# Linear attention and expert layer on one core: key features as the stationary side, z from a column of ones, logits from transposes, key subtractions on GpSimd

## The chip, the core and the metric

The kernel runs on one core of a Trainium2 chip. A core has a matrix engine (TensorE, PE; its weight loads are shown apart as PEld), a vector engine (VectorE, DVE), an engine for activations (ScalarE, ACT), a general one (GpSimd, POOL), and a queue engine (SyncE, SP) that issues most of the transfers between the device memory and the on-chip memory. Matrix products land in PSUM, eight banks of 128 x 512 f32. The engines run their own instructions in order and wait for each other by semaphores. The metric is the device time of one execution in microseconds.

## The reference

```python
def phi(x):
    proj = np.einsum('bhsd,df->bhsf', x, w_phi)
    proj = proj - np.max(np.abs(proj), axis=-1, keepdims=True)
    return np.concatenate([np.exp(proj), np.exp(-proj)], axis=-1)
q_p, k_p = (phi(q), phi(k))
kv = np.einsum('bhsf,bhsd->bhfd', k_p, v)
z = np.sum(k_p, axis=2)
num = np.einsum('bhsf,bhfd->bhsd', q_p, kv)
den = np.einsum('bhsf,bhf->bhs', q_p, z)[..., None] + 1e-06
attn = num / den                      # 8 batches, 8 heads, 576 tokens, 64 wide
x = attn.transpose(0, 2, 1, 3).reshape(4608, 512)
logits = x @ w_gate                   # 8 experts
...
out[mask] = np.maximum(x[mask] @ w1[e], 0.0) @ w2[e]
```

Projections have 128 features, so a head's feature vector has 256. The tokens are given to the experts in order of all logits, each expert taking at most 576; the left-out lines do that.

## The kernel before

The attention comes first, then the expert part (`moe`), whose instructions the change leaves alone. The attention has 16 units; a unit is two heads (a) of two batches (i). Its steps, with the names that the profile shows:

- SP loads keys and queries in pieces (ki, qi; eight transfers each) and values (vi; two transfers, one for each batch, with a row of 9 x 64 values in one piece). DVE transposes the 32 x 32 blocks (kT, qT, L158).
- Projection (L169): three groups of three token columns for keys and three for queries, each in a pair of PSUM banks. For each, DVE takes the maximum of the absolute values (kgm, qgm, L173) and subtracts it (kgt, qgt, L176), which frees the banks.
- Keys: ACT makes both exponentials (kP, L188). GpSimd adds kP up over the nine token columns (ks, L194 and L195), for z. PE multiplies (L204): the values are the stationary side, 64 x 64, and 256 features move past it. ACT copies the product (kvT, L208); PE multiplies it by a block that holds a unit matrix and the gate's weights (bd, L220), which turns it round and makes eight logit columns; ACT copies that into kz (L223). PE sums ks over the partitions (L235), and DVE copies the result into the 73rd column of kz (L237).
- Queries: PE transposes the features (L248), ACT makes the exponentials (qP, L252).
- Numerator (L265), in two halves g of five and four token columns: 73 columns, that is 64 values, 8 logits and the denominator. DVE divides (rd, xp, L269 to L280), SP stores xp into xs (L284), and GpSimd adds the logit columns into L (L290, L292); the last unit's are added by DVE.

Between them DVE makes constants (L353 to L414, of patterns that GpSimd makes) and, once a pair of batches is done, some steps of the routing (L424 to L478), with a count on PE (L474).

The order of all these steps is settled when the program is built: the class `Plan` is a list scheduler that knows for each step its engine, an estimated duration, the steps it needs, the buffers it takes and frees, and a due time. It takes the step with the earliest start on its engine and, among those ready, the one with the earliest due time, with an extra cost where PE would change its tile shape (mode). The due times are the unit's number times TI plus a constant for each kind of step, from the table ATT in the last lines. The step functions are then called in that order, so each engine's instructions stand in the planned order. PSUM is dealt out in four pairs of banks (kind 'g').

Of the kernel before, what the change touches and what calls it, by code (L numbers as in the profile page):

```python
# [89 lines left out]
def attention(ctx, tc, nc, q, k, v, w_phi, w_gate, xs, L, C, xp, cfg={}, after=None, later=None, count=None, init=iter(())):  # L90
# [24 lines left out]
    def loadv(u):  # L115
        bp,hp=divmod(u,NP)
        t=T['v',u]=sb.tile([128,2,9,D],F32,name='vi',bufs=2)
        for i in range(2):
            o=bass.AP(tensor=v.tensor,offset=v.offset+((2*bp+i)*H+2*hp)*HS,ap=[[9*D,64],[HS,2],[1,9*D]])
            nc.sync.dma_start(t[64*i:64*i+64].rearrange('p h s d -> p h (s d)'),o)  # L120
# [17 lines left out]
    def unit(u):  # L138
        bp,hp=divmod(u,NP)
        t0=u*d['TI']  # L140
        def add(name,eng,dur,due,fn,deps=(),mode=None,slot=(),frees=(),lat=None,after=0.):
            P.add((name,u),eng,dur,t0+due,fn,[(x,u) for x in deps],
                  lat={'PE':170.,'DVE':95.,'ACT':100.,'POOL':30.,'SP':0.}[eng] if lat is None else lat,mode=mode,slot=slot,frees=frees,after=after)
        def slots(*l): return tuple((kd,n,(kd,u) if len(z)==0 else (kd,u)+tuple(z)) for kd,n,*z in l)
        first=u==0
# [7 lines left out]
        def blocks(nm,aft):  # L153

            for bi in range(2):
# [3 lines left out]
                add((nm+'t',bi),'DVE',640.,d[nm+'t']+.7*bi,f,['ld'+nm],slot=slots((nm+'T',2)) if bi==0 else (),frees=((nm+'i',u),),after=aft[bi] if first else 0.)  # L159
        def project(nm,g,s0,s1,due,src):  # L160
# [13 lines left out]
            def sub(x):  # L174
                t=T[nm+'t',u,g]=sb.tile([128,2,n,128],F32,name=nm+'t',bufs=3)
                V.tensor_sub(t,vw(),T[nm+'m',u,g].to_broadcast([128,2,n,128]))  # L176
# [4 lines left out]
        blocks('k',(7500.,8500.))
        for g,(s0,s1) in enumerate(SG):
# [7 lines left out]
            def ad(x,s0=s0,s1=s1,g=g):  # L190
                if g==0: T['ks',u]=sb.tile([128,2,256],F32,name='ks',bufs=2)
                ks=T['ks',u]; kP=T['kP',u]
                for s in range(s0,s1):
                    if s==1: G.tensor_add(ks,kP[:,0],kP[:,1])  # L194
                    elif s>1: G.tensor_add(ks,ks,kP[:,s])  # L195
            add(('ad',g),'POOL',1300.*(n-(g==0)),due+4.,ad,[('ke',g)]+([('ad',g-1)] if g else []),frees=(('kP',u),),slot=slots(('ks',2)) if g==0 else ())
            def kv(x,s0=s0,s1=s1,g=g):
                if g==0: T['kvp',u]=pair(('g',u,'kv'))(x)
                p=T['kvp',u]; kP=T['kP',u]; v_=T['v',u]
                for s in range(s0,s1):  # L200
                    for i in range(2):
                        r=slice(64*i,64*i+64)
                        for a in range(2):
                            PE.matmul(p[64*a:64*a+64,i,0:256],v_[r,a,s,:],kP[r,s,a,:],start=s==0,stop=s==8,skip_group_check=True)  # L204
            add(('kv',g),'PE',n*430.+40.,d['kv']+d['kvs']*g,kv,[('ke',g)]+([('kv',g-1)] if g else ['ldv']),'Q',slots(('g',NG,'kv')) if g==0 else (),(('kP',u),('vi',u)))
        def kvt(x):
            t=T['kvT',u]=sb.tile([128,2,256],F32,name='kvT',bufs=2)
            A.copy(t,T['kvp',u][:,:,0:256])  # L208
        kend=d['kv']+2*d['kvs']+1.5
        add('kvt','ACT',ac(512),kend,kvt,[('kv',2)],frees=(('g',u,'kv'),))  # L210
        def bd(x):
            p=T['bdp',u]=pair(('g',u,'bd'))(x)
            t=T['kvT',u]
            for i in range(2):
                for fh in range(2):
                    for a in range(2):
                        r=slice(64*a,64*a+64)
                        for c in range(2):
                            o=128*fh+64*c
                            PE.matmul(p[64*c:64*c+64,a,72*(2*i+fh):72*(2*i+fh)+72],t[r,i,o:o+64],C['bd'][r,hp,:],start=True,stop=True)  # L220
        def kz(x):
            t=T['kz',u]=sb.tile([128,2,2,2,73],F32,name='kz',bufs=2)
            A.copy(t.rearrange('p i h a e -> p a (i h) e')[:,:,:,0:72],T['bdp',u][:,:,0:288].rearrange('p a (g e) -> p a g e',e=72))  # L223
        add('bd','PE',520.,kend+d['bd'],bd,['kvt'],'Q',slots(('g',NG,'bd')))
        add('kz','ACT',ac(576),kend+d['bd']+.6,kz,['bd'],slot=slots(('kz',2)),frees=(('g',u,'bd'),))
        def z(x):
            p=T['zp',u]=pair(('g',u,'z'))(x)
            ks=T['ks',u]
            for a in range(2):
# [26 lines left out]
        for g,(j0,j1) in enumerate(JG):  # L256
# [9 lines left out]
            def dve(x,g=g,j0=j0,j1=j1,n=n):  # L266
# [7 lines left out]
                if lastu:  # L274
                    V.tensor_mul(x_[:,:,j0:j1,64:72],p[:,:,:,64:72],rd.to_broadcast([128,2,n,8]))
# [637 lines left out]
```

## Time and profile before

| | |
|---|---|
| median of 3 runs | 811.54 us (810.16 to 812.07) |
| the profiled execution | 809.45 us, its span 807.7 us |
| PE busy | 756.6 us (94% of the span) |
| DVE busy | 573.1 us (71%) |
| ACT busy | 327.3 us (41%) |
| POOL busy | 263.8 us (33%) |
| mean granted clock of PE | 0.975 |

Busy times are counted over the whole span, in which the attention takes a good third; a share of the whole says little about one of the two parts. In the rows of the timeline and of the groups, L and a number is a line of the kernel, the names behind the operation are the tile written and those read, and x and a number is the count of instructions. A matrix product in f32 shows two records for each call in the code, so a group of 12 calls is shown as x24; the transposes show one. [...]

### The profile page before, as it was taken

What the parts mean: (1) busy time and instruction counts of PE and PEld (TensorE: products, weight loads), DVE (VectorE), ACT (ScalarE), POOL (GpSimd) and SP (SyncE); (2) the same over time, 40 slices, a digit from 0 to 9 for tenths busy, and PEclk for the clock granted to TensorE, in tenths of its full rate; (3) what the DMA queues carried; (4) which work ended last, traced back from release to release, by engine and by line L of the source; (5) the groups of instructions that cost most, each with busy time, mean ns of one, the idle gap of its engine ahead of it and who ended that gap; (6) DMA issues with size and microseconds to landing.
All of it is one profiled execution on the core that took longest, in us unless ns stands there. A gap on an engine that the chain in (4) does not pass through costs nothing.

```text
span 807.7 us, 25190 instructions
## 1 busy us (share of the span) xinstructions
PE 756.6 (94%) x10718; PEld 653.4 (81%) x10718; DVE 573.1 (71%) x1407; ACT 327.3 (41%) x579; POOL 263.8 (33%) x295
## 2 busy tenths in 40 slices
PE   5888999999999996799999999999999999999995
PEld 3777887888888785488798798798898898897983
DVE  5798899999999885787686686586586685550400
ACT  2544555665554463143343243234334333441410
POOL 2664676655666560200401302203103104302011
PEclk9999999999999997699999999999999999999998
DMA  8868668668777311433424314405314424701300
GB/s 130 146 119 161 119 121 155 128 118 165 126 152 143 77 33 32 134 135 116 128 83 144 127 58 161 161 16 180 138 54 137 138 89 131 271 1 45 119 27 32
DMA packets 225344, 91.89 MB, mean 114 GB/s; under 512 B 191905, under 2 KB 208321, under 8 KB 225233
## 3 DMA queue, kind: packets, MB, share of 16 engines
q1 hardware_dynamic: 214400, 70.74, 37.5%
q0 software_dynamic: 6096, 18.97, 7.0%
q8 instruction: 84, 1.38, 0.7%
q10 hardware_dynamic: 4736, 0.59, 0.5%
q14 instruction: 28, 0.22, 0.1%
HBM read 71.39 MB, written 18.87 MB: 112 GB/s over the span
## 4 chain that ended last, share of the span: by engine, by line
PE 58%; issue 14%; DVE 10%; POOL 5%; SPq 5%; DMA 4%; ACT 3%; POOLq 0%; DVEq 0%; ACTq 0%
PE h L788 19%; PE y L817 17%; PE g L265 5%; SPq L114 4%; PE g L204 3%; PE g L169 3%; POOL ks L195 3%; PE y L832 2%; PE g L248 2%; ACT qP L252 2%; DMA qi<-in_q_dram 2%; PE h L763 2%; POOL out_dram L846 1%; PE rps L541 1%; DMA ki<-in_k_dram 1%
## 5 line engine op out<-in xcount | busy, mean ns | idle before, releaser
L195 POOL TENSOR_TENSOR ks<-ks,kP 128x512 f32<-128x512 f32 x112 | 142.8, 1275 | 9.9 <-ACT kP L188 1.3
L788 PE MATMUL h<-xh,w1h 128*128 128x272 f32 (+3 forms) x512 | 144.5, 303 | 0.2 <-DVE xl L766 0.2
L788 PE MATMUL h<-xh,w1l 128*128 128x272 f32 (+3 forms) x512 | 143.0, 299 | 0.0
L846 POOL DMA_INDIRECT out_dram<-ysb,idx x40 | 40.4, 1010 | 206.2 <-ACT ysb L840 166.7
L799 ACT ACTIVATE fh<-h 128x272 fp32r<-128x272 f32 (+2 forms) x128 | 49.2, 384 | 134.8 <-PE h L788 123.6
L817 PE MATMUL y<-w2h,fl 128*128 128x512 f32 x256 | 102.2, 399 | 0.0
L817 PE MATMUL y<-w2l,fh 128*128 128x512 f32 x256 | 101.9, 398 | 0.0
L817 PE MATMUL y<-w2h,fh 128*128 128x512 f32 x256 | 101.5, 397 | 0.0
L788 PEld LDWEIGHTS h<-xh,w1h 128*128 128x128 f32 x512 | 96.5, 189 | 2.1 <-issue 1.2
L758 POOL DMA_INDIRECT xg<-xs,idx x40 | 39.5, 987 | 177.2 <-issue 141.3
L788 PEld LDWEIGHTS h<-xh,w1l 128*128 128x128 f32 x512 | 96.7, 189 | 0.0
L803 DVE SCALAR_TENSOR_TENSOR fl<-h,fh 128x272 fp32r<-128x272 f32 (+2 forms) x128 | 52.8, 420 | 55.8 <-ACT fh L799 42.4
L788 PE MATMUL h<-xl,w1h 128*128 128x272 f32 (+3 forms) x512 | 91.8, 298 | 0.0
L188 ACT ACTIVATE kP<-kgt 128x768 f32<-128x768 f32 x96 | 74.5, 835 | 32.9 <-DVE kgt L176 32.5
L265 PE MATMUL g<-kz,qP 128*64 128x73 f32 x2304 | 77.6, 227 | 3.9 <-issue 2.1
L265 PEld LDWEIGHTS g<-kz,qP 128*64 128x64 f32 x2304 | 74.9, 136 | 7.6 <-issue 4.2
L252 ACT ACTIVATE qP<-g 128x768 f32<-128x768 f32 x96 | 71.9, 820 | 11.2 <-PE g L248 11.1
L788 PEld LDWEIGHTS h<-xl,w1h 128*128 128x128 f32 x512 | 75.6, 189 | 0.0
L204 PE MATMUL g<-kP,vi 64*64 64x256 f32 x1152 | 69.7, 382 | 2.4 <-DVE xp L280 1.3
L840 ACT COPY ysb<-y 128x512 f32<-128x512 f32 (+1 forms) x40 | 21.8, 544 | 101.1 <-PE y L817 70.9
L204 PEld LDWEIGHTS g<-kP,vi 64*64 64x64 f32 x1152 | 48.1, 135 | 13.8 <-issue 2.1
L194 POOL TENSOR_TENSOR ks<-kP 128x512 f32<-128x512 f32 x16 | 20.5, 1280 | 109.2 <-ACT kP L188 109.2
(179 smaller groups left out, 1329.2 us busy)
## 6 DMA issues: line engine op xcount, KB each, us to landing
raww<-in_moe_w_dram SPq DMA_DIRECT2D x64, 512.0 KB, 6.2
vi<-in_v_dram SPq DMA_DIRECT2D x32, 288.0 KB, 4.6
xs<-xp SPq DMA_DIRECT2D x32, 288.0 KB, 3.8
ki<-in_k_dram SPq DMA_DIRECT2D x124, 72.0 KB, 3.2
qi<-in_q_dram SPq DMA_DIRECT2D x124, 72.0 KB, 3.3
xg<-xs,idx POOLq DMA_INDIRECT x40, 3.6
out_dram<-ysb,idx POOLq DMA_INDIRECT x40, 3.5
ki<-in_k_dram ACTq DMA_DIRECT2D x4, 72.0 KB, 5.3
```

Source lines behind the costliest of these rows:

```text
L114: eng.dma_start(t[64*a+32*db:64*a+32*db+32,bi],o)
L188: for i in range(2): A.activation(o[:,:,:,128*i:128*i+128],t,AF.Exp,scale=1.0-2*i)
L195: elif s>1: G.tensor_add(ks,ks,kP[:,s])
L204: PE.matmul(p[64*a:64*a+64,i,0:256],v_[r,a,s,:],kP[r,s,a,:],start=s==0,stop=s==8,skip_group_check=True)
L252: for fh in range(2): A.activation(t[:,fh].rearrange('p a s t -> p a (s t)'),p,AF.Exp,scale=1.0-2*fh)
L265: PE.matmul(p[64*ab:64*ab+64,a,73*(j-j0):73*(j-j0)+73],T['qP',u,j//3][:,fh,a,j%3,64*ab:64*ab+64],T['kz',u][:,ab,fh,a,:],start=fh==0,stop=f ...
L758: G.indirect_dma_start(out=T['xg',r][0:n,bb,:],out_offset=None,in_=xs,in_offset=bass.IndirectOffsetOnAxis(ap=T['idx',r][0:n,bb,:],axis=0))
L788: PE.matmul(p,ws[:,k,o:o+128],xx[:,k,o1:o2],start=n==0,stop=n==11)
L799: A.activation(hh[:,f,o1:o1+m1],p[:,0:m1],AF.Relu)
L803: V.scalar_tensor_tensor(hl[:,f,o1:o1+m1],p[:,0:m1],0.0,hh[:,f,o1:o1+m1],op0=OP.max,op1=OP.subtract)
L817: PE.matmul(p,hx[:,f,o:o+128],ws[:,f%2,:],start=n==0,stop=n==23)
L846: st=G.indirect_dma_start(out=ov,out_offset=bass.IndirectOffsetOnAxis(ap=iv,axis=0),in_=yv,in_offset=None)
```

## The change

The key-value product has its sides exchanged: the features kP are stationary, in 64 x 64 pieces, and the values move, 64 columns and a 65th of ones, so that z comes out with the product. It is made of four steps of 9 token columns (one for each half of the features and head), and the first now needs all three groups of kP. GpSimd's sums, the product with bd, the product for z and DVE's copy fall away. The ones stand in two fixed value tiles; the values are loaded in four transfers a unit, each with rows of 64 values in a piece.

The logit columns are made from the product in kz: PE transposes its four blocks (tv), ACT copies them (tc), PE multiplies them by the gate's weights (gl, 16 columns), and ACT copies the eight columns that belong to each head beside its values (gc). In kz the two heads of a block now share their neighbourhood of columns: logits, ones and values of the one (columns 0 to 72), values, ones and logits of the other (73 to 145), and the code behind it takes the denominator, values and logits from other columns.

The keys' subtraction of all three groups goes from DVE to GpSimd: ACT copies the projection from PSUM into kgt, DVE still takes the maximum from PSUM, and GpSimd subtracts in place.

```diff
-    def loadv(u):
+    def loadv(u,b):
         bp,hp=divmod(u,NP)
-        t=T['v',u]=sb.tile([128,2,9,D],F32,name='vi',bufs=2)
+        t=T['v',u]=VI[b]
         for i in range(2):
-            o=bass.AP(tensor=v.tensor,offset=v.offset+((2*bp+i)*H+2*hp)*HS,ap=[[9*D,64],[HS,2],[1,9*D]])
-            nc.sync.dma_start(t[64*i:64*i+64].rearrange('p h s d -> p h (s d)'),o)
+            for a in range(2):
+                o=bass.AP(tensor=v.tensor,offset=v.offset+((2*bp+i)*H+2*hp+a)*HS,ap=[[9*D,64],[D,9],[1,D]])
+                nc.sync.dma_start(t[64*i:64*i+64,a,:,1-a:1-a+D],o)
...
+            if (nm,g) in POOLS:
+                def cp(x):
+                    t=T[nm+'t',u,g]=sb.tile([128,2,n,128],F32,name=nm+'t',bufs=NT[nm])
+                    A.copy(t.rearrange('p a s f -> p a (s f)'),T[nm+'p',u,g][:,:,0:128*n])
+                def gs(x):
+                    t=T[nm+'t',u,g]
+                    G.tensor_sub(t,t,T[nm+'m',u,g].to_broadcast([128,2,n,128]))
...
-            def kv(x,s0=s0,s1=s1,g=g):
+        for g in range(4):
+            def kv(x,fh=g//2,a=g%2,g=g):
                 if g==0: T['kvp',u]=pair(('g',u,'kv'))(x)
                 p=T['kvp',u]; kP=T['kP',u]; v_=T['v',u]
-                for s in range(s0,s1):
-                    for i in range(2):
-                        r=slice(64*i,64*i+64)
-                        for a in range(2):
-                            PE.matmul(p[64*a:64*a+64,i,0:256],v_[r,a,s,:],kP[r,s,a,:],start=s==0,stop=s==8,skip_group_check=True)
+                for s in range(9):
+                    for i in range(2):
+                        r=slice(64*i,64*i+64)
+                        for c in range(2):
+                            o=128*fh+64*c
+                            PE.matmul(p[64*c:64*c+64,i,(D+1)*g:(D+1)*g+D+1],kP[r,s,a,o:o+64],v_[r,a,s,:],start=s==0,stop=s==8)
...
+        def tv(x):
+            p=T['lp',u]=pair(('g',u,'l'))(x); t=T['kz',u]
+            for j in range(4): PE.transpose(p[:,0,128*j:128*j+128],t[:,j//2,j%2,9:137],ident)
...
+        def gl(x):
+            p=T['lp',u]; t=T['kvT',u]
+            for j in range(4): PE.matmul(p[:,1,16*j:16*j+16],t[:,j],C['wg'][:,hp],start=True,stop=True)
...
-ATT = {'TI': 16.83, 'ldk': 65.46, 'ldq': 71.93, 'ldv': 49.44, 'kt': -9.67, 'kg': -1.7, 'ks': 1.44, 'kv': 7.1, 'kvs': 1.81, 'bd': -4.2, 'z': 0.71, 'qt': -5.11, 'qg': 4.92, 'qs': 1.97, 'T': 4.09, 'num': 17.7, 'ns': 3.45, 'stay': 3.02}
+ATT = {'TI': 13.41, 'ldk': 48.71, 'ldq': 62.94, 'ldv': 60.44, 'kt': -8.38, 'kg': -0.58, 'ks': 0.05, 'kv': 7.44, 'kvs': 1.81, 'qt': 1.7, 'qg': 6.14, 'qs': 2.98, 'T': 5.1, 'num': 17.25, 'ns': 11.76, 'stay': 5.85, 'Tv': -3.44, 'G': 2.09}
```

With the new table and the new steps the planner puts all of a unit into another order. The first place is one period of PE in the middle of the attention, before (g and a number is a pair of banks, the tile read tells the step):

```order
L265 MATMUL g_2961<-kz,qP 64x73 x40
L265 MATMUL g_3013<-kz,qP 64x73 x32
L169 MATMUL g_3057<-w,qT 64x128 x12
L169 MATMUL g_3085<-w,qT 64x128 x12
L204 MATMUL g_3100<-kP,vi 64x256 x12
L169 MATMUL g_3115<-w,qT 64x128 x12
L204 MATMUL g_3100<-kP,vi 64x256 x24
L248 MATMUL g_3163<-ident,qgt 128x128 x6
L248 MATMUL g_3177<-ident,qgt 128x128 x6
L220 MATMUL g_3190<-bd,kvT 64x72 x16
L235 MATMUL g_3218<-one,ks 64x2 x16
L169 MATMUL g_3238<-w,kT 64x128 x12
```

Behind these rows come a transpose group, two more key projections and the next unit's numerator. The same place of PE with the change:

```order
L214 MATMUL g_2849<-vi_95,kP 64x65 x108
L175 MATMUL g_2962<-w,qT 64x128 x12
L175 MATMUL g_2977<-w,kT 64x128 x12
L214 MATMUL g_2849<-vi_95,kP 64x65 x36
L175 MATMUL g_3032<-w,kT 64x128 x12
L175 MATMUL g_3054<-w,kT 64x128 x12
L223 MATMUL g_3071<-ident,kz 128x128 x4
L245 MATMUL g_3078<-ident,qgt 128x128 x6
L245 MATMUL g_3090<-ident,qgt 128x128 x6
L231 MATMUL g_3071<-wg,kvT 128x16 x4
L245 MATMUL g_3107<-ident,qgt 128x128 x6
```

Ahead of these rows stand two query projections; behind them come the second half of the former unit's numerator, the first half of this unit's, and the next unit's first two query projections. All products of 64 x 64 tiles now stand together, then all of 128 x 128, then both halves of numerators; the second half of a unit's numerator has moved behind the next unit's product.

The second place is ACT in the same period, with the change:

```order
L188 COPY kgt<-g_2977 128x768
L219 COPY kz<-g_2849 128x4x130
L188 COPY kgt<-g_3032 128x768
L188 COPY kgt<-g_3054 128x768
L227 COPY kvT<-g_3071 128x512
L249 ACTIVATE qP<-g_3078 128x768 x2
L235 COPY kz<-g_3071 128x4x8 x2
L249 ACTIVATE qP<-g_3090 128x768 x2
L203 ACTIVATE kP<-kgt 128x2x3x128 x6
L249 ACTIVATE qP<-g_3107 128x768 x2
```

Before, ACT's period was the exponentials of kP (x6), the copy kvT, two exponentials qP, the copy kz and four more qP. The three copies of the key projections and the two of logit columns are new, and the keys' exponentials now stand between the second and the third pair of the queries'.

The third place is the start of SP's queue, before:

```order
L114 DMA ki<-in_k_dram 32x18x32 x4
L114 DMA qi<-in_q_dram 32x18x32 x4
L120 DMA vi<-in_v_dram 64x2x576 x2
L114 DMA qi<-in_q_dram 32x18x32 x8
L114 DMA ki<-in_k_dram 32x18x32 x8
```

and with the change:

```order
L118 DMA ki<-in_k_dram 32x18x32 x4
L118 DMA qi<-in_q_dram 32x18x32 x4
L125 DMA vi_95<-in_v_dram 64x9x64 x4
L118 DMA qi<-in_q_dram 32x18x32 x8
L125 DMA vi_96<-in_v_dram 64x9x64 x4
L118 DMA ki<-in_k_dram 32x18x32 x8
```

The second unit's keys (the last row) have moved behind that unit's values, and both units' values are twice as many transfers.

More of the change, by code (lines that the diff above doesn't have):

```diff
@@ L105, in attention @@
     HS=S*D
+    VI=[sb.tile([128,2,9,D+1],F32,name='vi%d'%i,bufs=1) for i in range(2)]
+    ZC=(0,D); EC=(0,D+1); NC=(9,0)
+    for t in VI:
+        for a in range(2): V.memset(t[:,a,:,ZC[a]:ZC[a]+1],1.0)
     C.update(weights(ctx,tc,nc,w_gate,C))
@@ L140, in unit, with add @@
         t0=u*d['TI']
-        def add(name,eng,dur,due,fn,deps=(),mode=None,slot=(),frees=(),lat=None,after=0.):
+        def add(name,eng,dur,due,fn,deps=(),mode=None,slot=(),frees=(),lat=None,after=0.,seq=None):
             P.add((name,u),eng,dur,t0+due,fn,[(x,u) for x in deps],
-                  lat={'PE':170.,'DVE':95.,'ACT':100.,'POOL':30.,'SP':0.}[eng] if lat is None else lat,mode=mode,slot=slot,frees=frees,after=after)
+                  lat={'PE':170.,'DVE':95.,'ACT':100.,'POOL':30.,'SP':0.}[eng] if lat is None else lat,mode=mode,slot=slot,frees=frees,after=after,seq=seq and (seq,u))
         def slots(*l): return tuple((kd,n,(kd,u) if len(z)==0 else (kd,u)+tuple(z)) for kd,n,*z in l)
@@ L158, in f @@
                     V.transpose(T[nm+'T',u][:,bi].rearrange('p s t l -> p l s t'),T[nm,u][:,bi])
-                add((nm+'t',bi),'DVE',640.,d[nm+'t']+.7*bi,f,['ld'+nm],slot=slots((nm+'T',2)) if bi==0 else (),frees=((nm+'i',u),),after=aft[bi] if first else 0.)
+                add((nm+'t',bi),'DVE',640.,d[nm+'t']+.7*bi,f,['ld'+nm],slot=slots((nm+'T',2)) if bi==0 else (),frees=((nm+'i',u),),after=aft[bi] if first else 0.,seq=(nm+'t',0) if bi else None)
         def project(nm,g,s0,s1,due,src):
@@ L205, in unit @@
[L205 to L229, printed above, removed]
-                for fh in range(2):
+                for s in range(9):
@@ L259, in pe @@
             def pe(x,g=g,j0=j0,j1=j1):
[L260 removed]
+                p=T['np',u,g]=pair(('g',u,'num',g))(x).rearrange('p a c -> p (a c)')
                 for a in range(2):
@@ L331, in weights @@
     W=dict(C)
[L332 removed]
+    wg=cp.tile([128,4,2,8],F32,name='wg'); W['wg']=wg.rearrange('p h a e -> p h (a e)')
+    nc.gpsimd.memset(wg,0.0)
     g=w_gate.rearrange('(h a d) e -> a d h e',a=2,d=64)
[L334 to L337 removed]
+    for i in range(2): nc.gpsimd.dma_start(wg[64*i:64*i+64,:,i,:],g[i])
     return W
```

83 lines of the change are left out of this document (44 added, 39 removed).

## Prediction

> **What bounds the kernel now.** First the stages (us, busy time of PE, PE's weight loads, DVE, ACT and POOL with their instruction counts, granted clock, DMA share, GB/s), one stretch in the attention and one in the expert part:
> ```profile
> 100.00:200.00 100.00, 95.51 (x2523) 81.51 (x2516) 95.19 (x169) 57.93 (x81) 62.32 (x57) 1.00 0.73 135
> 400.00:500.00 100.00, 100.00 (x810) 88.74 (x807) 72.81 (x229) 36.07 (x77) 16.20 (x23) 1.00 0.36 119
> ```
> The expert part is TensorE's alone, and none of its instructions changes, so the sum is made over the attention. There PE and DVE are both 95% busy and ACT and POOL some 60%. Next, the numerator of one unit (two heads of two batches; 16 units in all) marks the period; the rows are pieces of the chain and of the timeline:
> ```profile
> 55.06 4.79 PE L265 MATMUL g<-kz,qP 128*64 128x73 f32 x144 [0.20 <-ACT qP L252]
> ...
> 164.77 4.79 PE g L265 x144
> ...
> 303.64 5.04 PE L265 MATMUL g<-kz,qP 128*64 128x73 f32 x144
> ```
> These are units 1, 7 and 15: (164.77 - 55.06)/6 = 18.3 us a unit early, (303.64 - 164.77)/8 = 17.36 us later. The attention ends at 303.64 + 5.04 = 308.7 us. 95% of 17.36 us is a need of **16.5 us a unit on DVE and as much on PE**; the rest is waiting for each other. Third, PE's timeline over one such unit (start, length, work):
> ```profile
> 218.09 4.79 PE L265 MATMUL g<-kz,qP 128*64 128x73 f32 x144 [0.37 <-DVE kgt L176]
> 222.81 1.54 PE L169 MATMUL g<-w,qT 64*64 64x128 f32 x48
> 224.17 1.48 PE L204 MATMUL g<-kP,vi 64*64 64x256 f32 x24
> 225.46 0.83 PE L169 MATMUL g<-w,qT 64*64 64x128 f32 x24
> 226.12 2.77 PE L204 MATMUL g<-kP,vi 64*64 64x256 f32 x48
> 228.82 1.53 PE L248 MATMUL g<-ident,qgt 128*128 128x128 f32 x12
> 230.28 0.73 PE L220 MATMUL g<-bd,kvT 64*64 64x72 f32 x32
> 230.83 0.59 PE L235 MATMUL g<-one,ks 64*64 64x2 f32 x32
> 231.35 0.89 PE L169 MATMUL g<-w,kT 64*64 64x128 f32 x24
> 232.17 0.88 PE L248 MATMUL g<-ident,qgt 128*128 128x128 f32 x6
> 232.98 1.54 PE L169 MATMUL g<-w,kT 64*64 64x128 f32 x48
> 234.84 2.38 PE L265 MATMUL g<-kz,qP 128*64 128x73 f32 x68 [0.32 <-DVE kgt L176]
> ```
> What counts is start to next start, since matmuls overlap: numerator 4.72, a projection group 0.66 (225.46 to 226.12), key-value product 1.29 + 2.70 = 3.99, block products 0.55, z 0.52, a transpose group 0.65 (1.46 for two less 0.81 for one). Where the tile shape changes, a group takes 0.16 more (0.82 against 0.66). Without the idle 0.32 at its end the unit is 16.43 us, six changes of shape in it.
>
> **The change on DVE.** Groups of the attention (busy us, mean ns):
> ```profile
> L173 DVE TENSOR_REDUCE kgm<-g 128x6 f32<-128x768 f32 x48 | 44.8, 948 | 4.5 <-PE g L169 4.1
> L176 DVE TENSOR_TENSOR kgt<-g,kgm 128x768 f32<-128x768 f32 x48 | 44.8, 951 | 2.0
> L237 DVE COPY kz<-g 128x8 f32<-128x8 f32 x15 | 2.3, 151 | 0.3 <-PE g L235 0.3
> L195 POOL TENSOR_TENSOR ks<-ks,kP 128x512 f32<-128x512 f32 x111 | 141.6, 1275 | 9.8 <-ACT kP L188 1.3
> L474 PE MATMUL g<-OH,cmp 128*32 128x8 bf16 x27 | 2.1, 203 | 0.7 <-DVE cmp L473 0.7
> ```
> The keys' subtractions (44.8 us) and the z copies (2.3) go: 47.1/16 = 2.9 us a unit, so DVE's need falls from 16.5 to **13.6 us** and it stops being a bound. What is late next is PE.
>
> **The change on PE.** Key-value product: 36 rounds of four 64x64 tiles (144 matmuls, two records each), 65 columns, where there were 256. The nearest rows have the same tile shape: four rounds of 72 columns in 0.55 us, four of 2 columns in 0.52 us. So 36 rounds are 9 x 0.52 = 4.7 us at most; less the start of a group (some 0.05 us in each row) 4.2. I take 4.3, against 3.99 before. Far above lies the numerator's price, 288 records in its 4.72 us for 144: 9.4 us. It is the price of 128x64 tiles, two side by side, so I leave it to a rival.
>
> [...]
>
> Out go block products and z, 1.07 us. In come four transposes, 4/6 of 0.65 = 0.43 us, and four logit products of 16 columns on 128x128 tiles, eight records. The latter has no row: as four transposes 0.43, as eight 0.87; I take 0.5, near the lower end, since 2 columns cost hardly less than 72 above. With the new order three shape changes are left, 0.48. New need: 4.72 + 6 x 0.66 + 3 x 0.65 + 4.3 + 0.43 + 0.5 + 0.48 = 16.34, and 0.16 for the count (three times 0.70 us): **16.5 us** (16.3 to 17.0). PE's own work thus hardly falls; what goes is DVE as a second full engine.
>
> **ACT and POOL.** Rows of ACT, whose paces are (length - one record)/(count - 1):
> ```profile
> 283.51 0.75 POOL L292 TENSOR_TENSOR L<-L,xp 128x72 f32<-128x72 f32 x2
> 284.02 0.58 ACT L208 COPY kvT<-g 128x512 f32<-128x512 f32 x1 [4.58 <-PE g L204]
> 286.78 2.95 ACT L252 ACTIVATE qP<-g 128x768 f32<-128x768 f32 x4
> 292.03 3.05 ACT L188 ACTIVATE kP<-kgt 128x768 f32<-128x768 f32 x4 [0.83 <-DVE kgt L176]
> ...
> 307.49 3.79 ACT L279 ACTIVATE xp<-g,rd 128x64 f32<-128x64 f32 x18 [1.35 <-DVE xp L275]
> ```
> 768 elements pace at (2.95 - 0.82)/3 = 0.71 us, keys at 0.735. Three new copies 2.1, keys 4.4, queries 4.3, two copies of about 500 at 0.5 each, two small ones at 3.79/18 = 0.21: 12.2 us, no bound by itself. POOL loses its 8 adds a unit (10.2 us) and gets three subtractions of 768: 1275 x 1.5 = 1.9 us each, 5.7, plus 0.75. Bounds 1.3 (as long as 512) and 2.5; either leaves it half idle.
>
> But they form a chain. From the end of the third key projection (0): the last key copy ends at 1.1 behind its predecessors, the block's copy 1.6, queries 3.1, logit copies 3.45, queries 4.9, keys 9.3. All three key groups must be there before the product starts now; before, one sufficed. PE meanwhile has 0.16 + 0.43 + 1.95 + 0.5 + 0.16 + 4.72 + 0.16 + 1.32 = 9.4 us. So the cover is almost exact; POOL's third subtraction, done at about 4.4, is covered by 3 us.
>
> **Start and sum.** The load queue (SP) issues four v transfers a unit in place of two, and unit 1's keys stand behind both v loads:
> ```profile
> 9.46 1.32 SPq L120 DMA_DIRECT2D vi<-in_v_dram  x2
> 10.82 6.26 SPq L114 DMA_DIRECT2D qi<-in_q_dram  x8
> 17.12 5.36 SPq L114 DMA_DIRECT2D ki<-in_k_dram  x8
> ...
> 25.08 0.78 DVE L158 STREAM_TRANSPOSE kT<-ki 128x576 f32<-128x576 f32 x1 [0.46 <-DMA ki<-in_k_dram]
> ...
> 33.60 4.79 PE L265 MATMUL g<-kz,qP 128*64 128x73 f32 x144
> ```
> At 0.66 an issue (1.32/2), six more issues move that 4 us: the transpose ends at about 29.9. Behind it on DVE stand a query maximum and subtraction and two transposes (3.3 us), the first key maximum (34.2), on POOL its subtraction (36.1), on ACT two key exponentials ahead of the logit copies (38): unit 0's numerator starts at **38.3** (36.8 to 40) instead of 33.6. The early units were slow (18.3 us against 17.36; the first two 21.5):
> ```profile
> 33.00:55.00 22.00, 18.89 (x462) 16.78 (x454) 18.81 (x42) 9.99 (x15) 15.63 (x19) 0.92 0.76 136
> ...
> 41.55 1.28 DVE L366 TENSOR_SCALAR kt<-ktf 128x128 bf16<-128x128 f32 x1 [2.54 <-POOL ktf L365]
> ```
> The granted clock is 0.92 there, and DVE waits for POOL's constants; both stay. Of some 9 us beyond the pace in the first units I keep 5 (3 to 8), as DVE now has room.
>
> Period: need 16.5, and half of the 0.86 that two full engines lose now: **16.9**. The last period has no keys ahead: 14.7 (16.9 less three key groups, 2.0, and less the count), then 4.9 for the last numerator. End: 38.3 + 14 x 16.9 + 14.7 + 4.9 + 5 = 299.5, against 308.7: **9.2 us less**. The profiled execution took 809.45, 2.1 below the median of 811.54; from the median, 802.3.
>
> **Rivals.**
> PE alone is the bound: period 16.4, start 36.8, early loss 3: 36.8 + 229.6 + 19.6 + 3 = 289, 19.7 less, 792 us. For it: DVE, ACT and POOL all get 2.5 us of room. Against: the chain above just fits.
>
> The ACT chain takes the place of DVE, slower than before. Place: from the third key projection to the next key-value product. With whole records (0.85 for a copy of 768, between 0.58 for 512 and half as much again; 0.58; 0.82 four times; 0.4; 0.835 six times; 0.4 left of an earlier copy) it takes 10.5, and hand-offs 0.4, an estimate from the numerator's waits of 0.37 and 0.32; product, one query and three key groups add 6.9: period 17.8, end 38.3 + 249.2 + 19.6 + 5 = 312.1, 3.4 more, 815. It decides from a period of (308.7 - 62.9)/14 = 17.56. Against it: the rows above pace faster than whole records.
>
> The load queue binds. Two units of SP, back to back:
> ```profile
> 158.10 8.40 SPq L114 DMA_DIRECT2D ki<-in_k_dram  x8
> ...
> 190.87 6.05 SPq L114 DMA_DIRECT2D ki<-in_k_dram  x8
> ...
> 264.56 1.35 SPq L120 DMA_DIRECT2D vi<-in_v_dram  x2
> ```
> 40 issues stand between the first two starts: 32.77/40 = 0.82 us each, or 18.0 for a unit's 22. The queue runs ahead, so only its total counts: 306 issues until 265.9, 0.866 each with its idle time; 336 at that rate end at 291, v lands 5 later and the last unit needs 15.8 (4.3 + 2 x 0.66 + 3 x 0.65 + 0.43 + 0.5, then 2.1 and 4.72 of numerators, and 0.5 of shape changes): 312, or 812 to 815 with the median; at 0.82 without idle, 297 and no loss. It would leave the time within 0.2% or just above.
> ```profile
> q1 hardware_dynamic: 2336, 0.59, 66.4%
> ...
> q1 hardware_dynamic: 361, 0.61, 41.9%
> ```
> The first row is 4 us with one store of 256-byte pieces (2.66 us of all engines), the second 6 us with one v load in 2304-byte pieces (2.51): cutting v's rows to 256 bytes costs the engines little. [...]
>
> Small matmuls issue one after another, at the numerator's 33 ns a record: +5.1 us on 16 units, some 80 us slower. The 2-column row speaks against it.
>
> **How the numbers follow.** Forecast 0.58, PE alone 0.17, queue 0.10 (0.07 within 0.2%, the rest slower), ACT chain 0.12, serial matmuls 0.03; 0.03 of the forecast's share ends within 0.2% (1.6 us, about what a measurement of this kernel tells from no change). So faster 0.72, same 0.10, slower 0.18. Range: 790, the PE case with a kindlier start, to 815, the ACT chain.
>
> **What would show it.** Right: numerators of units 7 and 15 135 us apart, DVE under 85% busy at 100 to 200 us, the new product at 4.2 to 4.5 us for 288 records, unit 0's numerator at 37 to 40, POOL's subtractions near 1.9 us, an end near 299. Wrong: the product waiting for ACT's keys in each unit (ACT chain), DVE's transposes waiting for loads (queue), or a product over 5 us.

## The result and the profile after

| | before | after |
|---|---|---|
| median | 810.85 us of 4 runs (809.18 to 812.07) | 877.57 us of 4 runs (876.57 to 881.03) |
| ratio, 95% interval | | 1.081 (1.077 to 1.0851) |
| span of the profiled execution | 807.7 us | 876.2 us |
| end of the attention | 308.7 us | 375.0 us |
| PE records | 10718 | 13342 |
| mean granted clock of PE | 0.975 | 0.963 |

The change makes the kernel 66.7 us slower; the forecast of 802 and its range up to 815 are missed by far. 66.4 us of the 68.5 in the spans stand in the attention, the rest in the expert part. Its windows after the change (the columns are those of the prediction's first fence):
```profile
100.00:200.00 100.00, 81.58 (x2662) 75.29 (x2660) 64.44 (x105) 55.48 (x87) 24.30 (x22) 0.98 0.60 110
200.00:300.00 100.00, 83.49 (x2857) 78.12 (x2852) 64.30 (x107) 55.20 (x85) 20.52 (x21) 0.97 0.61 112
```
No engine is full any more: PE fell from 95% to 82%, DVE from 95% to 64%, ACT and POOL have room, and the DMA engines are at 0.60. The clock, 0.97 to 0.98 for 1.00, is lower by 3% at most; if all of PE's work went with it, an estimate, that would be 3% of the time. So something that is no engine's work sets the pace. PE's timeline over one unit shows where PE stands still; the bracket is the idle time ahead of a row and what ended it. (Matrix records overlap: one of L214 lasts 229 ns in the mean, and within a run of them the next starts 16.5 ns later, so prices are taken from start to start.)
```profile
203.88 1.54 PE L175 MATMUL g<-w,qT 64*64 64x128 f32 x48
205.68 2.28 PE L214 MATMUL g<-vi,kP 64*64 64x65 f32 x138 [0.26 <-PE g L175]
210.23 1.33 PE L214 MATMUL g<-vi,kP 64*64 64x65 f32 x75 [2.27 <-issue]
...
212.66 0.22 PE L214 MATMUL g<-vi,kP 64*64 64x65 f32 x1
214.66 1.22 PE L214 MATMUL g<-vi,kP 64*64 64x65 f32 x68 [1.73 <-issue]
...
219.11 0.98 PE L245 MATMUL g<-ident,qgt 128*128 128x128 f32 x7 [0.72 <-issue]
219.93 0.96 PE L231 MATMUL g<-wg,kvT 128*128 128x16 f32 x8
220.74 0.86 PE L245 MATMUL g<-ident,qgt 128*128 128x128 f32 x6
221.53 4.79 PE L263 MATMUL g<-kz,qP 128*64 128x73 f32 x144
...
351.21 4.79 PE L263 MATMUL g<-kz,qP 128*64 128x73 f32 x144
...
368.23 6.82 PE L263 MATMUL g<-kz,qP 128*64 128x73 f32 x208
```
Between the rows at 221.53 and 351.21 lie six units: (351.21 - 221.53)/6 = 21.6 us each, against 17.36 before; the last row ends the attention at 375.05. In the one shown PE stops for 2.27, 1.73 and 0.72 us, and each time the bracket says "issue": the profile shows nothing that was waited for. Twice it stops in the midst of the key-value product, between two of its own records. While it runs, it runs as forecast: 138 records in 2.28 us are 16.5 ns each. From 100 to 300 us PE is idle for 34.9 us, and for 29.5 of them the profile names "issue". The page of the profile has the same in sum, and with it a row that the prediction passed over, the queue that the profile calls "instruction":
```profile
q8 instruction: 105, 1.72, 0.8%
...
L214 PE MATMUL g<-vi,kP 64*64 64x65 f32 x4608 | 88.6, 229 | 41.3 <-issue 37.4
L214 PEld LDWEIGHTS g<-vi,kP 64*64 64x64 f32 x4608 | 83.6, 143 | 47.3 <-issue 47.3
```
88.6 us busy and 41.3 idle are 8.1 us a unit for a product that was forecast at 4.3. The q8 row: 105 packets, 1.72 MB, so 16 KB each. PE has 13342 multiplications and as many weight loads, and 2 x 13342/105 = 254: **there is one packet to about 256 of PE's instructions, or 128 pairs** of a load and a multiplication. Before, the page of the profile had
```profile
q8 instruction: 84, 1.38, 0.7%
```
and 2 x 10718/84 = 255. Taken from 100 to 300 us alone, the same row (packets, MB, share) reads, before and then after the change:
```profile
q8 instruction: 40, 0.66, 1.3%
```
```profile
q8 instruction: 43, 0.70, 1.4%
```
That is a packet in 5.0 us before, with PE 95% busy, and one in 4.65 us after, with PE 82% busy: the change has made many more instructions necessary (606 pairs a unit for 442), and hardly more packets come (43 for 40).

The trace has the start of each packet. For the window above, the next list has the packets behind which PE paused: the packet's start, then the pause in PE's weight loads that begins before the next packet, if it is over 0.7 us (from the start of one load to the start of the next), and the number of that load in the program:
```
packet at 207.90; pause of 2.54 us from 207.69, load 5057
packet at 212.44; pause of 2.00 us from 212.66, load 5185
packet at 216.65; pause of 1.10 us from 218.01, load 5312
packet at 230.41; pause of 2.40 us from 230.48, load 5694
```
5185 - 5057 = 128, 5312 - 5185 = 127, and 5694 - 5312 = 382, three times some 127. PE pauses at fixed places of the program, 256 instructions apart: the trace also has PE's semaphore instructions, and when they are counted with the loads and multiplications, all 26 pauses of over 1 us named "issue" from 70 us to the end of the attention come behind 193 or 194 instructions of a block of 256. Waits for data or for another engine would hardly keep to such a count.

Where PE waits for one block after another, the packets follow at 4.54 (212.44 - 207.90) and 4.21 us (216.65 - 212.44). From one restart to the next, 16 blocks of the attention between two such pauses (of over 0.5 us) took 3.6 to 4.8 us, 4.2 in the mean; the two in this window took 4.4. That gives the theory, read from these counts and times: the instructions come in blocks of 128 pairs, and in this kernel the next block comes some 4.2 to 4.4 us behind the last. Whoever works a block off sooner waits for the next one. A unit had 442 pairs before (projections and numerator 144 each, product 72, block products and z 32 each, transposes 18), which is 3.45 blocks, or 15.2 us at 4.4, less than the 17.36 that it took. It has 606 now (product 288, new transposes 4, logits 8, block products and z gone): 4.73 blocks, 19.9 us at 4.2 and 20.8 at 4.4, near the 21.6 measured.

Two rivals were put beside this **theory 1**. **Theory 2**: the short matmuls themselves cost more than the short rows showed, so they slow down anywhere, at any place of the program. **Theory 3**: the chain over ACT and GpSimd, through which all three key groups now go ahead of the product, sets the pace.

### The profile page after: what moved, and what is told of

The parts are those of the page before. It is cut to its first block, busy times and chain, and to the rows that moved or that the text cites. A ratio compares the mean times of both kernels' runs of the same rounds, so it can differ in the third digit from the quotient of the medians.

```text
span 876.2 us, 30320 instructions
## 1 busy us (share of the span) xinstructions
PE 778.0 (89%) x13342; PEld 689.5 (79%) x13342; DVE 538.4 (61%) x1347; ACT 362.6 (41%) x659; POOL 171.4 (20%) x216
## 3 DMA queue, kind: packets, MB, share of 16 engines
q8 instruction: 105, 1.72, 0.8%
## 4 chain that ended last, share of the span: by engine, by line
PE 40%; issue 11%; POOL 2%; DVE 2%; DMA 1%; ACT 0%; POOLq 0%; SPq 0%; DVEq 0%; ACTq 0%
PE h L787 18%; PE y L816 16%; PE y L831 2%; PE h L762 1%; POOL out_dram L845 1%; PE rps L540 1%; PE rps L536 1%; DMA raww<-in_moe_w_dram 1%; POOL xg L757 1%; PE rps L624 0%; DVE cmp L524 0%; PE rps L554 0%; DVE cc L560 0%; DVE cmp L616 0%; DVE w1l L745 0%
## 5 line engine op out<-in xcount | busy, mean ns | idle before, releaser
L214 PE MATMUL g<-vi,kP 64*64 64x65 f32 x4608 | 88.6, 229 | 41.3 <-issue 37.4
L214 PEld LDWEIGHTS g<-vi,kP 64*64 64x64 f32 x4608 | 83.6, 143 | 47.3 <-issue 47.3
L191 POOL TENSOR_TENSOR kgt<-kgt,kgm 128x768 f32<-128x768 f32 x48 | 70.2, 1473 | 214.9 <-DVE kgm L179 198.5
L188 ACT COPY kgt<-g 128x768 f32<-128x768 f32 x48 | 37.3, 801 | 134.6 <-PE g L175 122.4
L179 DVE TENSOR_REDUCE qgm<-g 128x6 f32<-128x768 f32 x48 | 45.6, 950 | 46.7 <-PE g L175 46.7
L203 ACT ACTIVATE kP<-kgt 128x768 f32<-128x768 f32 x96 | 72.6, 860 | 1.9 <-POOL kgt L191 1.9
```

What stands on the lines that cost most here:

```text
L179: V.tensor_reduce(m,vw(),axis=AX.X,op=OP.max,apply_absolute_value=True)
L191: G.tensor_sub(t,t,T[nm+'m',u,g].to_broadcast([128,2,n,128]))
L203: for i in range(2): A.activation(o[:,:,:,128*i:128*i+128],t,AF.Exp,scale=1.0-2*i)
L214: PE.matmul(p[64*c:64*c+64,i,(D+1)*g:(D+1)*g+D+1],kP[r,s,a,o:o+64],v_[r,a,s,:],start=s==0,stop=s==8)
```

## Experiments

The kernels of the first six headings ran once each, so a difference of a few microseconds between them counts for little; the last four kernels ran 4 or 10 times. The edits are shown shortened, and 65 stands for D+1 of the code.

### The product's matmuls alone

No kernel at all: streams of matmuls on four 64x64 tiles, from operands that are there from the beginning. One stream for each width; 92 key loads run beside the first 74 us.
```diff
+for n,cnt in ((65,128),(256,64),(65,128),(2,128),(72,128),(128,128),(256,64)):
+    for j in range(cnt):
+        for i in range(2):
+            for c in range(2): PE.matmul(P[64*c:64*c+64,i,0:n],ST[64*i:64*i+64,64*c:64*c+64],MV[64*i:64*i+64,0:n],start=True,stop=True)
```


> The cost by itself: nothing of the reference is computed, only streams of f32 matmuls of 64x64 tiles, one after another without a wait: 65, 256, 65, 2, 72, 128 and 256 columns; key loads run beside the first two. Theory 1 (TensorE's instructions come in blocks of 16 KB, that is 128 load-and-multiply pairs, and a block takes some 4.4 us to come with loads running and 3.6 without, requested when the one before is entered): bursts of 128 pairs at 14 to 16 ns each, then a gap; 65, 2 and 72 columns all take 26 to 30 ns a pair on average without loads and some 34 with them; 128 columns (27 ns a pair by their columns) about 28; 256 columns 54 ns a pair, no gap. Theory 2 (small matmuls of four tiles have a pace of 14 to 16 ns, and the gaps in the changed kernel come from its buffers, waits or accumulation): 65, 2 and 72 columns at 14 to 16 ns a pair throughout, no gaps.

The time is 211.52 us. PE's timeline in the second stream of 65 columns, with loads (the first two rows) and without, and in that of 72 with the beginning of the next:
```profile
65.58 2.09 PE L36 MATMUL pp<-mv,st 64*64 64x65 f32 x128 [1.84 <-issue]
69.85 2.09 PE L36 MATMUL pp<-mv,st 64*64 64x65 f32 x128 [2.18 <-issue]
...
81.86 2.09 PE L36 MATMUL pp<-mv,st 64*64 64x65 f32 x128 [1.63 <-issue]
85.59 2.09 PE L36 MATMUL pp<-mv,st 64*64 64x65 f32 x128 [1.64 <-issue]
...
144.69 2.23 PE L36 MATMUL pp<-mv,st 64*64 64x72 f32 x128 [1.50 <-issue]
148.15 21.27 PE L36 MATMUL pp<-mv,st 64*64 64x72 f32 x768 [1.23 <-issue]
```
DVE, ACT and POOL have no work (0.00 us busy from 60 to 93 and from 125 to 172 us), and yet PE does exactly 128 pairs in 2.09 us (16.3 ns each), stops for 1.6 to 2.2 us, and does the next 128: one block in 3.73 (85.59 - 81.86) to 4.27 us. The same instructions that need 2.09 us in a burst can't be slow in themselves, so theory 2 falls in its plain form. The stream of 72 columns comes in the same bursts to its end: from 119.47 to 148.70 us it takes 28.5 ns a record. The last row bears the form of its first records, but only some 33 of its 768 have 72 columns; the rest have 128, of which 128 records last 3.72 us, about as long as a block needs, and the pauses left between them are 0.28 us. (The stream of 2 columns ran at a granted clock of 0.54 and is left out.)

### Short and long ones mixed

The same streams once more, without loads: 384 records of 65 columns and then 384 of 256, three times; and then the same number and kinds, 16 of the one and 16 of the other by turns. More records of 65 columns stand ahead and behind.
```diff
+for rep in range(3): stream(65,48); stream(256,48)
+for rep in range(72): stream(65,2); stream(256,2)
```


> Streams alone again, no loads beside them: three times 384 pairs of 65 columns and then 384 pairs of 256 columns; after that the same 2304 pairs (1152 and 1152), but mixed, 16 of the one and 16 of the other in turn; then 1024 pairs of 65 columns. Theory 1 (a block of 128 pairs takes some 3.7 us to come, requested when the one before is entered, so that only one block is ahead): the separate form has gaps of 1.6 to 2 us in each stretch of 65 columns, two or three a stretch, some 26.7 us of work and 4 to 6 us of gaps for each 768 pairs; the mixed form none, 80 us in all against 92 to 98. If more than one block were fetched ahead, the stretches of 65 columns behind the slow ones would start without a gap for as many blocks.

Of one separate stretch, and of all the mixed part:
```profile
51.66 2.09 PE L36 MATMUL pp<-mv,st 64*64 64x65 f32 x128 [1.30 <-issue]
55.39 24.68 PE L36 MATMUL pp<-mv,st 64*64 64x65 f32 x640 [1.64 <-issue]
...
85.04 103.77 PE L36 MATMUL pp<-mv,st 64*64 64x65 f32 x2944 [1.91 <-issue]
190.72 2.09 PE L36 MATMUL pp<-mv,st 64*64 64x65 f32 x128 [1.91 <-issue]
```
A row of the timeline can hold both widths: that of 640 records is 33 short ones, 384 of 256 columns and 223 short ones. That of 2944 is the end of the last separate stretch (417 records), the mixed part and 223 short records behind it, all without a pause. By the records' starts, the 2304 of the three separate stretches take 91.8 us, the 2304 mixed ones 79.0, that is 34.3 ns a pair or 4.4 us a block. Theory 1 had given 92 to 98, and 80: the same short matmuls go without a pause where a block as a whole lasts longer than its successor needs to come. Behind the long records 223 short ones pass before the first pause: the rest of a block (95) and 128, so one block, and no more, was there ahead of time. When a block is asked for, no run shows.

### The changed kernel with half the records

The product as 72 matmuls with a 64x128 stationary side in place of 144 with 64x64: 462 pairs a unit.
```diff
-for c in range(2):
-    o=128*fh+64*c
-    PE.matmul(p[64*c:64*c+64,i,65*g:65*g+65],kP[r,s,a,o:o+64],v_[r,a,s,:],start=s==0,stop=s==8)
+PE.matmul(p[:,i,65*g:65*g+65],kP[r,s,a,128*fh:128*fh+128],v_[r,a,s,:],start=s==0,stop=s==8)
```


> The changed kernel, but the key-value product takes stationary pieces of 64 rows and 128 columns: 72 matmuls a unit for 144, same result, same order of everything. Theory 1 (instruction supply): 144 pairs fewer a unit is 1.1 blocks or some 4.9 us less supply; the product itself gets longer (7 us for 4.2 of stream) but has no gap; period 19 to 20.5 for 21.8, time 835 to 860. Theory 2 (waits or the work of the small matmuls): the product's stream gets longer by 3 us and nothing else changes, so the time grows to 900 or more.

891.64 us: above what theory 1 gave (835 to 860), and nearer to what was put down for theory 2 (900 or more). One window, and the product of one unit:
```profile
200.00:300.00 100.00, 97.59 (x2078) 91.94 (x2077) 64.40 (x107) 57.81 (x91) 24.17 (x22) 0.98 0.58 107
```
```profile
213.58 6.25 PE L212 MATMUL g<-vi,kP 64*128 64x65 f32 x108 [0.27 <-DMA qi<-in_q_dram]
...
219.76 0.89 PE L175 MATMUL g<-w,qT 64*64 64x128 f32 x24
...
221.23 2.23 PE L212 MATMUL g<-vi,kP 64*128 64x65 f32 x36
```
The pauses are gone, as they must be by theory 1: from 100 to 300 us no wait of PE is named "issue" (29.5 us in the changed kernel), and PE is 98% busy. But 108 records take 6.18 us from start to next start (219.76 - 213.58), 57 ns each, where 64x64 records go at 16; the numerator's 128x64 records of 73 columns go at 33. The product is 8.3 us a unit again, this time as work. The miss is in the price of this form, which I had put at 7 us; whether two such tiles work side by side at all, the run doesn't show. By its time the run doesn't help theory 1; the missing pauses are what speaks for it.

### The changed kernel with more work in the same records

Three quarters of the product's matmuls get 130 columns in place of 65 (each value column twice, the second half into columns of the bank that nobody reads). The number of records stays.
```diff
-PE.matmul(p[64*c:64*c+64,i,65*g:65*g+65],kP[r,s,a,o:o+64],v_[r,a,s,:],start=s==0,stop=s==8)
+q_=p[64*c:64*c+64,i,65*g:65*g+65]; m_=v_[r,a,s,:]
+if g<3:
+    q_=bass.AP(tensor=q_.tensor,offset=q_.offset,ap=[list(q_.ap[0]),[260,2],[1,65]])
+    m_=bass.AP(tensor=m_.tensor,offset=m_.offset,ap=[list(m_.ap[0]),[0,2],[1,65]])
+PE.matmul(q_,kP[r,s,a,o:o+64],m_,start=s==0,stop=s==8)
```


> The changed kernel, but three of the four steps of the key-value product have 130 moving columns for 65 (the ones and values twice, the second copy into unused columns of the bank, which nobody reads): same result, same instructions, 2.8 us more of work a unit on TensorE by the columns. Theory 1 (instruction supply): the work fills the gaps, time 870 to 890. Theory 2 (TensorE's work or waits bound the period): 16 x 2.8 = 45 us more, some 920.

883.45 us. The window, and the product of one unit:
```profile
200.00:300.00 100.00, 92.56 (x2774) 87.12 (x2776) 64.86 (x108) 56.61 (x89) 21.26 (x22) 1.00 0.61 112
```
```profile
207.12 4.20 PE L218 MATMUL g<-vi,kP 64*64 64x130 f32 x138 [0.26 <-DMA qi<-in_q_dram]
211.67 2.34 PE L218 MATMUL g<-vi,kP 64*64 64x130 f32 x75 [0.35 <-issue]
...
215.94 1.22 PE L218 MATMUL g<-vi,kP 64*64 64x65 f32 x68 [0.51 <-issue]
```
138 records now last 4.20 us, not 2.28, and the pause behind them is 0.35, not 2.27: the next records start 4.55 us after the first, as they did before (210.23 - 205.68). PE's share rises by 9 points, its waits named "issue" fall from 29.5 to 11.3 us between 100 and 300 us, and the kernel takes some 6 us more, 0.4 us a unit. **Almost twice the work in the product is nearly free, since it fills time in which the next block was under way.** That is a plain sign that in the changed kernel the count of instructions sets the pace, not their work.

### The changed kernel without its GpSimd part

All key subtractions back on DVE.
```diff
-pools=(('kg',0),('kg',1),('kg',2))
+pools=()
```


> The changed kernel with all subtractions on VectorE again, without the copies and GpSimd (the planner makes its order anew). Theory 1 (instruction supply): VectorE needs 16.6 us a unit, TensorE's supply still some 21: time 865 to 890, as with the change. Theory 3 (the chain over ACT's copies, GpSimd and the exponentials costs the time): back to 800 to 830.

903.85 us, 26 more than the changed kernel. So theory 3 falls: without the chain over GpSimd the time doesn't come back to 800 to 830. It is also more than theory 1 gave (865 to 890). The window shows that PE is as little busy as before, at a lower clock:
```profile
100.00:200.00 100.00, 81.18 (x2454) 75.38 (x2457) 67.57 (x109) 40.65 (x64) 2.32 (x7) 0.90 0.54 98
```
From 100 to 300 us PE waits 27.6 us by "issue" (29.5 in the changed kernel), so the supply is as short as there. On top of it come 10.0 us in which it waits for DVE's subtractions (5.6) and for ACT (4.4), where the changed kernel has 0.5. That is some 1.2 us a unit (a unit takes 23.8 here), or 19 of the 26 us if it is the same in all units; the granted clock of 0.90 and the planner's other order weren't separated from it.

### The kernel before with more records

The 16 small z matmuls, two records each, nine times over: 442 + 256 = 698 pairs a unit, and nothing else of the change.
```diff
+for rep in range(9):
   for a in range(2):
```


> The kernel before with nine times the z products (288 pairs of 2 columns a unit for 32; the result is the same, eight of the nine are thrown away). Theory 1 (instruction supply): 256 pairs more are two blocks, some 7.5 to 9 us a unit where the products stand in one row, so 16 x 7 to 8: 900 to 945, with gaps marked issue in that line or 27 to 34 ns a pair. Theory 2 (small matmuls run at 14 to 16 ns a pair): 16 x 3.9 = 62 us less what VectorE's bound hides, 850 to 875.

951.54 us, 141 more than before, which is 8.8 us a unit or 34.5 ns for each of the 256 added pairs. The z part of one unit:
```profile
220.88 2.22 PE L236 MATMUL g<-one,ks 64*64 64x2 f32 x143
224.54 3.26 PE L236 MATMUL g<-one,ks 64*64 64x2 f32 x128 [1.45 <-issue]
228.82 0.69 PE L236 MATMUL g<-one,ks 64*64 64x2 f32 x17 [1.02 <-issue]
```
The pauses appear in the kernel before as soon as it has as many instructions, again 128 records apart. 8.8 us for two blocks would be 4.4 us a block. But the granted clock is 0.83 and 0.82 in the windows from 100 to 300 us, where it was 1.00 before, and what that adds wasn't separated; the time lies above both ranges, that of theory 1 (900 to 945) and that of theory 2 (850 to 875). So the size is no measure. What the run shows is the place of the pauses.

### The GpSimd part alone

In the kernel before, one or two of the three key groups go over ACT's copy and GpSimd's subtraction, with product, z and block as they were; in a third kernel all three do, with the changed kernel's due times.
```diff
+POOLS=(('kg',0),)                       # e_before_gp1
+POOLS=(('kg',0),('kg',1))               # e_before_gp2
+POOLS=(('kg',0),('kg',1),('kg',2))      # e_gp3_new_table, with ATT as after the change
```


> The GpSimd part of the change alone: the kernel before with the first of the three key groups of a unit copied by ScalarE and subtracted by GpSimd, its own table of due times. 0.95 us a unit less on VectorE, the instructions of TensorE unchanged in number. Theory 1 (the instruction supply of the new product is the loss, the GpSimd part is sound): 798 to 811. Theory 3 (the copies and GpSimd make waits): 815 or more.

> The same with two of the three key groups: 1.9 us a unit less on VectorE; GpSimd has 10.2 us of adds and 3 of subtractions in a unit. Theory 1: 795 to 812. Theory 3: 820 or more.

> The kernel before with only the GpSimd part of the change, for all three key groups, and the changed kernel's table for the order (block products in the place of the new transposes); key-value product, block products and z as before, so 442 pairs a unit, as before. Theory 1: no shortage of instructions, so the period is that of the engines: PE 16.4, DVE 13.6, GpSimd 10.2 + 3 x 1.47 = 14.6 us; 795-825 us, that is at most 2% from before. Rival (the GpSimd chain is what makes the changed kernel slow): period 20 us or more, above 850 us.

They take 819.12, 819.73 and 819.17 us: ratios of 1.0112 (1.0088 to 1.0135), 1.0127 (1.0107 to 1.0146) and 1.0093 (1.007 to 1.0117). Slower by about one per cent each, however many groups move; for the first two I had expected no loss from theory 1 (798 to 811, 795 to 812), and the first lies in the range put down for theory 3 (815 or more). So this part does cost something, but one per cent and not eight. The window of the third, to be held against 95.51 for PE and 95.19 for DVE before:
```profile
100.00:200.00 100.00, 94.68 (x2479) 81.87 (x2472) 84.43 (x132) 64.82 (x91) 84.62 (x73) 0.95 0.73 135
```
DVE got 11 points of room, and PE's share stayed where it was, at a clock of 0.95 for 1.00. That speaks for PE, with its 16.4 us of work a unit, as the bound of the kernel before, and for DVE as only full beside it; the lower clock and the chain weren't separated from it. The prediction's "half of the 0.86 that two full engines lose" was not to be had this way. As the cause of the 66.7 us, theory 3 is excluded a second time.

### The change without its many records

This run decides between the theories. The changed kernel, all of it, only that the product streams its columns in the old form: 36 matmuls of 256 columns in place of 144 of 65, and four small ones; 398 pairs a unit. The columns that stream are nearly as many (36 x 256 = 9216 for 144 x 65 = 9360).
```diff
-PE.matmul(p[64*c:64*c+64,i,65*g:65*g+65],kP[r,s,a,o:o+64],v_[r,a,s,:],start=s==0,stop=s==8)
+st=v_[r,c,s,0:64] if s==8 else kP[r,s,c,192:256]
+PE.matmul(p[64*c:64*c+64,i,0:256],st,kP[r,s,c,:],start=s==0,stop=s==8,skip_group_check=True)
```


> The changed kernel with one thing different: the key-value product's columns stream in the old form, 36 matmuls of 256 columns a unit (72 records) in place of 144 of 65 columns (288 records), and 4 small ones fill the last 4 columns. It multiplies the key features with themselves, so the output isn't the reference's; all else of the change (copies on ACT, subtractions on GpSimd, transposes, logit products, order, loads) stays. Load-and-multiply pairs a unit fall from 606 to some 398, 3.1 blocks of instructions at 4.4 us = 13.7 us. Theory 1 (instruction supply is what the changed kernel lost): the period falls from 21.8 to 16.4-17.6 us, the attention ends at 290-310 instead of 374.8, the time is 790-815 us, the waits of 1.3-2.3 us on nothing that the profile shows go. Rival (the changed kernel's ACT and GpSimd chain, its loads or its order would have cost the time anyway): the period stays at 20 us or more and the time above 850.

816.65 us, 1.0071 (1.0042 to 1.01) of before, 1.65 above what theory 1 gave. **60.9 of the 66.7 us are gone with the records**, and the attention ends at 305.51 + 6.82 = 312.3 us in place of 375.0 (290 to 310 was expected):
```profile
100.00:200.00 100.00, 98.38 (x2309) 88.89 (x2307) 83.54 (x146) 71.05 (x112) 29.28 (x27) 1.00 0.73 132
200.00:300.00 100.00, 94.78 (x2180) 85.02 (x2177) 75.20 (x125) 65.40 (x101) 25.20 (x25) 0.97 0.65 120
```
```profile
93.79 4.79 PE L267 MATMUL g<-kz,qP 128*64 128x73 f32 x144
...
196.81 4.79 PE L267 MATMUL g<-kz,qP 128*64 128x73 f32 x144
...
290.59 4.79 PE L267 MATMUL g<-kz,qP 128*64 128x73 f32 x144
...
305.51 6.82 PE L267 MATMUL g<-kz,qP 128*64 128x73 f32 x208
```
PE is 98% busy from 100 to 200 us, where it had 82%, and from 100 to 300 us no wait of PE is named "issue". The rest of the change, the chain, the loads in small pieces and the transposes, costs 5.9 us by itself and gains nothing: in the spans 3.6 us in the attention and 3.6 in the expert part, whose instructions are the same. A version that beats the kernel before was not among these runs.

## Why the prediction was wrong

**The step that failed** is the first of the part on PE: "36 rounds are 9 x 0.52 = 4.7 us at most ... I take 4.3". The pace was right (128 pairs in 2.09 us would make 288 take 4.7), and the product took 8.1 us a unit, the prediction's own sign of being wrong ("a product over 5 us"). The rows from which it was priced hold 32 records each. That is a quarter of a block of instructions, and the groups around them take longer a record (projections 27.5 ns, transposes 108). No wait ahead of the two is named "issue" in the kernel before (block products: 0.0 us idle to 300 us; z: 5.1 us, behind DVE and POOL), and in the mixed stream above no group of 16 short ones waited. What a short row shows is the pace in a burst, and I carried it over to 288 records in a row. The sum that was left out: 606 pairs a unit, 4.73 blocks at 4.4 us, 20.8 us, against a forecast period of 16.9. It could have been made blind in part: the page of before has 84 packets for 2 x 10718 instructions, so 255 in one, and a packet came every 5.0 us in the attention, three times in 200 us as soon as 3.7 us behind another. If what was seen there was also the limit, the period is 4.73 x 3.7 = 17.5 to 4.73 x 5.0 = 23.7 us. A rival that ends up to (23.7 - 17.36) x 16 = 100 us slower belonged there.

That there is a limit could be seen in the trace of before as well:
```profile
180.83 1.10 PE L169 MATMUL g<-w,kT 64*64 64x128 f32 x32 [0.50 <-issue]
181.86 3.26 PE L265 MATMUL g<-kz,qP 128*64 128x73 f32 x95
185.98 1.75 PE L265 MATMUL g<-kz,qP 128*64 128x73 f32 x49 [0.86 <-issue]
```
Two pauses named "issue" stand 127 records apart (32 + 95), the second in the midst of a numerator that has all its operands. From 250.63 us it comes again (0.31 us, then 1.20 us behind 127 records), and all four lie behind 193 or 194 instructions of a block of 256, as after the change. They are 2.9 of the 8.9 us for which PE is idle from 100 to 300 us; the prediction had put all of that down to engines waiting for each other ("the rest is waiting for each other"). The price of a block couldn't be had from them: from restart to restart they give 5.2 and 5.5 us, more than the packets that came 3.7 us apart.

The runs bear out the size of a block: one packet of 16 KB came to 254 of PE's instructions in the changed kernel (2 x 13342/105), 255 before, 256 in the bare streams (2 x 6144/48) and 254 with half the records (2 x 11038/87). The mixed stream shows one block ahead of time (223 records, 95 + 128, without a pause). With matmuls this short that doesn't hide the wait: 1.6 to 2.2 us in every 3.7 to 4.3 stand open in the rows of 65 columns shown above.

**The rival of small matmuls issued one after another** (+80 us) comes near in time (+66.7), but not in its mechanism: records go at 16 ns, not 33, and the loss sits in pauses at fixed places.

Point by point, by the prediction's list:

- *DVE's need 13.6 us*: 64.4% of 21.6 is 13.9. Right.
- *DVE, then PE as the bound; a period of 16.9*: wrong in the changed kernel (21.6). With the old stream form and PE at 98%, the rows with the numerators of units 3 and 9 start at 93.79 and 196.81, 17.2 us a unit; of the gain of 0.46 that I forecast 0.2 is there, and from unit 9 to 14 (290.59) the units take 18.8. DVE's room by itself gained nothing in the third GpSimd kernel.
- *Logits at 0.5 us*: 0.81 (220.74 - 219.93), near the upper end of 0.87. Eight records of 128x128 tiles with 16 columns cost nearly as much as eight transposes.
- *POOL's subtraction 1.9 us (1.3 to 2.5)*: 1.47, within the bounds.
```profile
L191 POOL TENSOR_TENSOR kgt<-kgt,kgm 128x768 f32<-128x768 f32 x48 | 70.2, 1473 | 214.9 <-DVE kgm L179 198.5
```
- *Unit 0's numerator at 38.3 (36.8 to 40)*: 42.2. Two delays are together as large as the miss. Unit 1's second key transpose, which waits for its load, ends at 31.43 + 0.78 = 32.2, forecast 29.9; and PE's planned order has a query projection of 48 records between the logits and the numerator, 1.47 us that I left out. A pause of 0.81 named "issue" lies on the way too:
```profile
39.73 1.03 PE L231 MATMUL g<-wg,kvT 128*128 128x16 f32 x8 [0.81 <-issue]
40.69 1.54 PE L175 MATMUL g<-w,qT 64*64 64x128 f32 x48
42.16 2.76 PE L263 MATMUL g<-kz,qP 128*64 128x73 f32 x80
```
- *The ACT chain and the load queue as rivals*: neither binds in the changed kernel. In the old stream form, where PE is full again, a trace of the queue is seen: DVE holds a quotient back for an earlier store, which was issued on SP among the loads,
```profile
203.28 0.92 DVE L285 TENSOR_TENSOR xp<-g,rd 128x730 f32<-128x730 f32 x1 [1.21 <-DMA xs<-xp]
```
and DVE loses 3.3 us in this way from 100 to 300 us. PE waits 3.4 us behind it. That is about as much as the attention ends later than before (3.6 us); whether it is the cause wasn't tried.

**What stays open**: why a block takes 3.5 to 3.7 us in one place and 4.2 to 4.8 in another (the bare stream had 3.73 as well as 4.0 both with and without loads beside it; a cause wasn't separated), and why the rest of the change, with PE full, is slightly slower than the kernel before.

## What to carry to other kernels

Count PE's instructions in a period, not only their time: here each 128 pairs of load and multiplication took at least 3.46 us in a bare stream of short matmuls and some 4.2 us in the kernel, so over stretches longer than a block 27 to 34 ns a pair was the floor. Cutting a matmul into four with a quarter of the columns can therefore double its time (here from 3.99 to 8.1 us) though every record is nearly as fast as hoped. A duration from a row of a few dozen records held here for a few dozen (16 to 17 ns each in the rows of 32) and not for 288 (28 ns each); before it is multiplied to hundreds, look at the row of the instruction queue, and at pauses whose releaser is "issue" and which come 128 pairs apart; the kernel before already had four of them.

## What the runs showed of the hardware that was not expected

- The supply of PE's instructions: bursts of 128 pairs of 65 columns in 2.09 us, one in 3.5 to 4.3 us, with no other engine at work (the bare streams). In the changed kernel the pauses keep to one place in every 256 instructions, PE's semaphore instructions counted.
- 64x128 tiles took 57 ns a record at 65 columns (the product with half the records), against 16 for four 64x64 tiles: 3.5 times as long for twice the outputs.
- GpSimd subtracted 768 elements of a broadcast operand in 1473 ns, 1.9 ns an element, where its additions of 512 took 1275 ns, 2.5 ns each.
